# Sigmoid attention and a mixer MLP on one core: the third batch's cycles take the form of the later ones

## The chip, the core and the metric

The kernel runs on one core of a Trainium2 chip. The core has five engines that run side by side and meet at semaphores: TensorE (PE in the profile), which multiplies matrices and writes PSUM; VectorE (DVE) and ScalarE (ACT), which read PSUM and SBUF and compute element by element; GpSimd (POOL) and SyncE (SP), which here mostly start transfers. SBUF and PSUM have 128 partitions; PSUM holds eight banks of 512 f32 columns in each. The metric is the device time of one execution in microseconds (us); the median of several runs is given with its lowest and highest.

A matrix product here is written `matmul(out, lhsT, rhs)`: the weights `lhsT` are loaded into the array (at most 128 rows by 128 columns), then `rhs` streams through. Products of 64 rows by 64 columns occupy one quadrant of the array, and four of them in different quadrants run at once. The profile writes `64*64` or `128*128` for the two forms.

## The reference

Eight batches, twelve heads, 448 tokens, head size 64. Sigmoid attention, then one token-mixing and one channel-mixing MLP, each with a residual:

```python
scores = scale * np.matmul(q, k.transpose(0, 1, 3, 2)) - np.log(S)
attn = 1.0 / (1.0 + np.exp(-scores))
x = matmul(attn, v)                      # (8, 448, 768): heads side by side
h = np.maximum(x.transpose(0, 2, 1) @ w_tok1, 0.0) @ w_tok2   # over tokens, 256 wide
u = x + h.transpose(0, 2, 1)
out = u + np.maximum(u @ w_ch1, 0.0) @ w_ch2                  # over channels, 1536 wide
```

## The kernel before, in words

**Cycles.** The order of all instructions is written out by hand (a manual schedule); each engine executes its own instructions in that order. The unit of attention work is a *cycle* c = 3 b + u: batch b and one third u of its heads (four heads, in two groups g). There are 24 cycles, numbered from 0. A cycle holds seven score products `qk` (L179), each followed by a sigmoid on ACT (L191), and, one cycle later, the seven value products `av` (L201), whose result DVE casts into `xT` (L220) and SP transposes into `xn` by DMA (`xtrans_dma`, L235). Two cycles later the token MLP of that unit runs: `tok_tail` (L260) for the last 64 tokens, `tok1` (L278) for the other 384, a relu on ACT for each of its two halves (L303), and `ytrans` (L305), which multiplies by the second weight and adds x on DVE to give u, kept transposed in `uts`.

**Channel MLP.** Batch 0's first channel product (`ch1`) is spread over cycles 3 to 5. From batch 1 on it is `sevens` (L1049): seven products of sums and differences in place of eight plain ones, at the end of the third cycle of the next batch. It needs sums of the weight `c1` (`weight_sums`, L401: twelve DVE additions) and differences of u (`token_sums`, L422: four). Its seven products for three groups of outputs are named in `ORDER` (L1046); "2b" is the third step, and `banks` gives the banks for the single ones. The second channel product gives the output. Its 448 tokens are three blocks t of 128 and a last 64 (`ch2_last`, L722); each block has two halves of the 768 channels. A *group* is (t, half): twelve matmuls of 384 columns. For batch 0 the residual u is added on PE by three more matmuls with the identity (L552); for later batches u is transposed by DMA (`utrans`, L324) and added on DVE.

**Two forms of a cycle.** Cycles 6 to 8 (batch 2) are the loop at L1065. It puts batch 0's groups in whole-array form between the scores, a few matmuls at a time, from a list of pieces (`pending`) shared out by width (`work`, L1076). Cycles 9 to 23 are the loop at L1130. There a cycle's two groups, the two halves of one block of the batch two before, are a pair (`ch2_pair`, L582): eight of the twelve steps of both are done in quadrants (`quads`, L359), where the two row halves of the array work on different groups at a time and swap in the second turn, and the last four whole (`rest`, L602). So scores, pair, values and `tok_tail` are all 64x64 until the seventh score, and what follows (`tok1`, `rest`, `ytrans`, and in a batch's third cycle `ch2_last` and `sevens`) is 128x128.

**PSUM banks.** Scores and the larger products of `sevens` use two buffers of two banks each ("qk"). The other four banks, m0 to m3, are given out by `bank` (L85): in the opening by the string `OPENING_BANKS`, afterwards from `at_bank` upwards. The second loop gives the pair X = 2 and 3, and the values, then `tok_tail` and `tok1`, then `ytrans`, Y = 0 and 1; `ch2_last` takes Y + 1. In the first loop groups and `ch2_last` take 2 or 3. A tile that reuses a bank waits until its last reader is done.

**Queues.** `through_dma` (L144) prepares a batch's keys and queries: three DVE copies (`relayout`, L126) and one DMA transpose on SP for each. Such pieces wait in the list `copies`, and the loops take some of them off at set places (`some`, L1058; `within` and `behind` say how many). SP issues in order: transposes of x, keys, queries and u, and the stores of finished outputs (L577). POOL issues the loads. `gated_loads` (L969) lets POOL wait, by a copy that reads the transposed queries, before it loads keys, queries and values of later batches.

The opening, cycle 5 (L989) included, has its own loop; cycle 5 ends with two of batch 0's groups, (0, 0) and (1, 0), in whole-array form:

```python
for w, f in pieces_ch2(0, by_half[:2]):
    f()
    if copies:
        copies.pop(0)()
```

Of the kernel before, what the change touches and what calls it, by code (L numbers as in the profile page):

```python
# [10 lines left out]
FP32 = mybir.dt.float32  # L11
ADD = mybir.AluOpType.add
# [11 lines left out]
NU = 3  # L24
NS = 224
BY_GROUP = [0, 1, 6, 7, 2, 3, 8, 9, 4, 5, 10, 11]
OPENING_BANKS = "201301301301302130213021302130213130212130213021302021302"


@with_exitstack  # L30
def kernel(
# [53 lines left out]
    def bank(shape, dtype, name):  # L85

        if opening_banks:
            n = opening_banks.pop(0)
        else:
            n = at_bank[0]  # L90
            at_bank[0] = (n + 1) % 4
        return pp.tile(shape, dtype, tag=f"m{n}", bufs=1, name=name)
# [486 lines left out]
                in_=outs[b, t][64 * par : 64 * par + 64, :],  # L579
            )  # L580

    def ch2_pair(b, t):  # L582


        outs[b, t] = pa.tile([128, D], FP32, tag="outs", bufs=3, name=f"o_{b}_{t}")
        ps = [bank([128, 512], FP32, f"c2_{b}_{t}_{p}") for p in range(2)]
        n_quads = 8

        def step(turn, n):
            quads(  # L590
                ps,
                DH,
                turn,
                lambda p, part, m: h2[b][
                    part, BY_GROUP[n], 128 * t + m : 128 * t + m + 64
                ],
                lambda p, part: c2[part, BY_GROUP[n], DH * p : DH * p + DH],
                n == 0,
                False,
            )  # L600

        def rest():  # L602
            for p in range(2):
                for n in range(n_quads, NCB):
                    nc.tensor.matmul(  # L605
                        out=ps[p][:, 0:DH],
                        lhsT=h2[b][:, BY_GROUP[n], 128 * t : 128 * t + 128],
                        rhs=c2[:, BY_GROUP[n], DH * p : DH * p + DH],
                        start=False,
                        stop=(n == NCB - 1),  # L610
                    )
                ch2_out(b, t, p, ps[p])

        turns = [[lambda t=t, n=n: step(t, n) for n in range(n_quads)] for t in range(2)]
        return turns[0], turns[1], rest

    LOW, HIGH = slice(0, NCB // 2), slice(NCB // 2, NCB)
    D1, D2 = slice(0, DH), slice(DH, D)
# [234 lines left out]
    def pieces_ch2(b, groups):  # L853
        for t, half in groups:
            for n in range(0, NCB, 3):
                yield 3 * DH, lambda t=t, half=half, n=n: ch2(b, t, half, n, n + 3)

    def pieces_last(b):
        for n in range(0, NCB, 3):
            yield 3 * DH, lambda n=n: ch2_last(b, n, n + 3)  # L860
# [122 lines left out]

    ON_DMA = range(N_FIRST, N_CYCLES)

    ONE_RUN = 3 * NU

    by_half = sorted(((t, half) for t in range(3) for half in range(2)), key=lambda g: g[1])
    for c, cb in ((N_FIRST, 3), (N_FIRST + 1, 8)):  # L989
        b, u = divmod(c, NU)  # L990
        before = divmod(c - 1, NU)
        ahead = divmod(c + 1, NU)
        copies = []

# [24 lines left out]
        end()  # L1019
        qk(b, u, 6)  # L1020
        if u == 2:
            copies = by_unit(2, 1)
        whole(cb + 2)
        if c - 1 not in ON_DMA:
            xtrans(*before)
        for t in ("k", "q"):
            pe_transpose(ahead[0], t, ahead[1])
        whole(cb + 3)
        if c == N_FIRST:
            tok1(*before)  # L1030
            whole(cb + 4)
            nc.gpsimd.dma_start(out=w1[64:128, 3, :], in_=tok_rows[NJ - 1])
            ytrans(*before)
        else:
            for w, f in pieces_ch2(0, by_half[:2]):
                f()
                if copies:
                    copies.pop(0)()
            while copies:
                copies.pop(0)()  # L1040

            nc.gpsimd.tensor_copy(out=gate[:, :], in_=tr[2, "q"][:, 1, NJ - 1, 126:128])
            load(2, "v", v, 1, NU)
            gated_loads(b)
# [8 lines left out]
            if copies and at in (1, 3):  # L1053
                copies.pop(0)()

    pending, copies = [], []

    def some(n):  # L1058
        for f in copies[:n]:
            f()  # L1060
        del copies[:n]

    early = weight_sums()
    lane = [0]
    for c in range(2 * NU, ONE_RUN):  # L1065
        b, u = divmod(c, NU)
        before, ahead = divmod(c - 1, NU), divmod(c - 2, NU)


        if c == 2 * NU:  # L1070
            first = c
            pending, shares = [*pieces_ch2(0, by_half[2:]), *pieces_last(0)], [10, 10, 10]
            total = sum(w for w, f in pending)
            spent = 0

        def work(share):  # L1076
            goal = 3 * sum(shares[: c - first]) + share * shares[c - first]
            done = 0
            while pending and spent + done < total * goal / 90:
                w, f = pending.pop(0)  # L1080
                if len(pending) % 4 == 3:
                    lane[0] ^= 1
                at_bank[0] = 2 + lane[0]
                f()
                done += w
                if copies:
                    copies.pop(0)()
                elif early:
                    early.pop(0)()
            return done  # L1090

        some(len(copies))
        qk(b, u, 0)
        qk(b, u, 1)
        at_bank[0] = 0
        av(*before)
        xtrans_dma(*before)
        qk(b, u, 2)
        if c == 2 * NU + 2:
            copies += through_dma(3, 0)[NU + 1 :]  # L1100
        spent += work(1)
        qk(b, u, 3)
        qk(b, u, 4)
        if u < 2:
            at_bank[0] = 0
            tok_tail(*ahead)
            tok1(*ahead, with_scores=True)
        spent += work(2)
        if c == 2 * NU + 2:
            utrans(b - 1)  # L1110
            token_sums(b - 1)
        qk(b, u, 5)
        qk(b, u, 6)
        at_bank[0] = 0
        if u < 2:
            ytrans(*ahead)
        else:
            tok_tail(*ahead)
            tok1(*ahead, with_scores=True)
        if c == 2 * NU + 1:  # L1120
            copies += through_dma(3, 0)[: NU + 1]
        spent += work(3)
        if u == 2:
            sevens(b - 1)
            at_bank[0] = 0
            ytrans(*ahead)
            gated_loads(b)
    assert not copies and not pending and not early

    for c in range(ONE_RUN, N_CYCLES):  # L1130
        b, u = divmod(c, NU)
        before, ahead = divmod(c - 1, NU), divmod(c - 2, NU)
        if b == NU:
            within, behind = ((0, 0), (4, 2), (2, 0))[u]
        else:
            within, behind = ((0, 2), (2, 4), (0, 0))[u] if b < B - 1 else (2, 2)
        if u == 0:
            assert not copies
            copies += through_dma(b + 1, 0) if b + 1 < B else output_sums()

        X, Y = 2, 0
        at_bank[0] = X
        turn0, turn1, rest = ch2_pair(b - 2, u)
        part = len(turn1) * 2 // 3
        qk(b, u, 0)
        qk(b, u, 1)
        for f in turn0:
            f()  # L1150
        qk(b, u, 2)
        some(within)
        if c == ONE_RUN + 2:
            gated_loads(b)
        if u == 2:
            utrans(b - 1)
        at_bank[0] = Y
        av(*before, 0, 4)
        qk(b, u, 3)
        av(*before, 4, NJ)  # L1160
        xtrans_dma(*before)
        if u == 2:
            token_sums(b - 1)
        qk(b, u, 4)
        for f in turn1[:part]:
            f()
        qk(b, u, 5)
        for f in turn1[part:]:
            f()
        at_bank[0] = Y  # L1170
        tok_tail(*ahead)
        qk(b, u, 6)
        tok1(*ahead, with_scores=True)
        rest()
        if u == 2:
            at_bank[0] = Y + 1
            for w, f in pieces_last(b - 2):
                f()
            sevens(b - 1)
# [98 lines left out]
```

## Time and profile before

| What | Value |
|---|---|
| Median of 3 runs | 347.22 us (346.83 to 348.2) |
| The profiled execution | 347.06 us, span 345.3 us, granted TensorE clock 0.998 |
| PE busy | 337.6 us, 98% of the span |
| DVE busy, ACT busy | 213.3 us (62%), 210.5 us (61%) |
| POOL busy | 56.8 us (16%) |
| Cycle 5, from its first score matmul to that of cycle 6 | 50.95 to 64.03 us |
| Cycle 6 | 64.03 to 72.47 us |
| Cycle 7 | 72.47 to 81.08 us |
| Cycle 8, to the first of the seven products | 81.08 to 89.25 us |
| Seven products and `ytrans`, to cycle 9 | 89.25 to 102.18 us |
| Cycle 9 | 102.18 to 110.48 us |

The span goes from the first to the last instruction; the device time is a little longer. In the rows of the timeline the first number is the start, the second the length of the merged group, then engine, line, operation, what is written from what, the array form for matmuls, the shape, and the number of instructions; a bracket gives the idle time before and what ended it. Matmuls are pipelined and their ends are modelled, so a group's length runs into the next one: times between starts are the better measure. A line can be that of a helper.

### The profile page before, as it was taken

What the parts mean: (1) busy time and instruction counts of PE and PEld (TensorE: products, weight loads), DVE (VectorE), ACT (ScalarE), POOL (GpSimd) and SP (SyncE); (2) the same over time, 40 slices, a digit from 0 to 9 for tenths busy, and PEclk for the clock granted to TensorE, in tenths of its full rate; (3) what the DMA queues carried; (4) which work ended last, traced back from release to release, by engine and by line L of the source; (5) the groups of instructions that cost most, each with busy time, mean ns of one, the idle gap of its engine ahead of it and who ended that gap; (6) DMA issues with size and microseconds to landing.
All of it is one profiled execution on the core that took longest, in us unless ns stands there. A gap on an engine that the chain in (4) does not pass through costs nothing.

```text
span 345.3 us, 10253 instructions
## 1 busy us (share of the span) xinstructions
PE 337.6 (98%) x4465; PEld 238.5 (69%) x4465; DVE 213.3 (62%) x427; ACT 210.5 (61%) x271; POOL 56.8 (16%) x98
## 2 busy tenths in 40 slices
PE   7999999999999999999999999999999999999994
PEld 4555556555886669766896669766896669767962
DVE  2376466578574664657574664666665675976662
ACT  3996847488648865788448865688448875111400
POOL 8982440130040003000400004000100000000000
PEclk9999999999999999999999999999999999999999
DMA  8999999999999999969999999958992592035406
GB/s 127 158 170 194 209 203 203 173 185 233 199 180 194 189 172 206 164 104 168 182 155 175 161 163 209 184 104 159 178 146 34 78 173 66 1 78 129 78 2 159
DMA packets 104380, 52.17 MB, mean 151 GB/s; under 512 B 76432, under 2 KB 101264, under 8 KB 104336
## 3 DMA queue, kind: packets, MB, share of 16 engines
q1 hardware_dynamic: 78944, 29.70, 47.4%
q0 software_dynamic: 25168, 21.50, 42.1%
q8 instruction: 35, 0.57, 0.6%
q10 hardware_dynamic: 224, 0.33, 0.3%
q14 instruction: 9, 0.07, 0.1%
HBM read 43.45 MB, written 11.01 MB: 158 GB/s over the span
## 4 chain that ended last, share of the span: by engine, by line
PE 86%; DMA 5%; POOL 4%; ACT 2%; issue 1%; DVE 0%; ACTq 0%; POOLq 0%
PE c_ab L491 14%; PE c L367 12%; PE qk L184 8%; PE c_c L491 8%; PE xa L211 7%; PE c L541 6%; PE c L605 6%; PE yt L312 5%; PE tk L289 5%; PE c L734 5%; PE c L695 4%; DMA c<-in_moe_w_ch_dram 3%; PE c L344 3%; ACT att L191 2%; DMA w2s<-in_moe_w_tok_dram 2%
## 5 line engine op out<-in xcount | busy, mean ns | idle before, releaser
L191 ACT ACTIVATE att<-qk,att_bias 128x896 f16<-128x896 f32 x168 | 154.9, 1016 | 34.0 <-PE qk L184 33.6
L184 PE MATMUL qk<-tr_q,tr_k 64*64 64x448 f16 x672 | 58.1, 359 | 0.9 <-ACT att L191 0.6
L491 PEld LDWEIGHTS <-c 128*128 128x128 f16 x504 | 47.8, 98 | 1.9 <-issue 1.8
L220 DVE CAST xT<-xa 128x448 f16<-128x448 f32 x48 | 27.8, 620 | 32.5 <-PE xa L211 32.5
L367 PE MATMUL c<-c,h 64*64 64x384 f16 x960 | 46.6, 322 | 0.0
L211 PE MATMUL xa<-att,raw_v 64*64 64x448 f16 x672 | 39.5, 349 | 0.0
L512 ACT ACTIVATE pt_ab<-c_ab 128x896 f32<-128x896 f32 x21 | 19.3, 917 | 31.4 <-PE c_ab L491 30.2
L367 PEld LDWEIGHTS <-h 64*64 64x64 f16 x960 | 28.1, 107 | 11.9
L491 PEld LDWEIGHTS <-sum 128*128 128x128 f16 x378 | 36.3, 98 | 0.0
L184 PEld LDWEIGHTS <-tr_k 64*64 64x64 f16 x672 | 20.5, 105 | 20.7 <-issue 13.0
L564 DVE TENSOR_TENSOR o<-un,c 128x384 f32<-128x384 f16 x34 | 18.8, 554 | 23.8 <-PE c L605 20.4
L319 DVE TENSOR_TENSOR ut<-xT,yt 128x448 f16<-128x448 f16 x48 | 27.5, 615 | 3.0 <-PE yt L312 3.0
L211 PEld LDWEIGHTS <-raw_v 64*64 64x64 f16 x672 | 20.2, 107 | 10.9 <-issue 0.3
L971 POOL COPY gate<-tr_q 128x2 f16<-128x2 f16 x6 | 1.1, 190 | 153.5 <-DMA tr_q<-rel_q 153.5
L303 ACT ACTIVATE h<-tk 128x256 f16<-128x256 f32 x42 | 14.4, 415 | 14.8 <-PE tk L289 14.8
L541 PE MATMUL c<-c,h 128*128 128x384 f16 x120 | 22.3, 326 | 0.0
L312 PE MATMUL yt<-w,h 128*128 128x448 f16 x96 | 22.1, 353 | 0.0
L605 PE MATMUL c<-c,h 128*128 128x384 f16 x120 | 22.0, 326 | 0.0
L514 ACT ACTIVATE h<-c_ab 128x896 f16<-128x896 f32 x7 | 6.4, 917 | 24.4 <-PE c_ab L491 24.4
L289 PE MATMUL tk<-xn,w 128*128 128x256 f16 x156 | 21.2, 274 | 0.1
L521 DVE TENSOR_TENSOR h<-pt_ab,c_ab 128x896 f16<-128x896 f32 x14 | 15.2, 1084 | 9.6 <-PE c_ab L491 9.6
L521 DVE TENSOR_TENSOR h<-pt_c,c_c 128x448 f16<-128x448 f32 x21 | 13.0, 617 | 12.4 <-PE c_c L491 12.4
(100 smaller groups left out, 458.7 us busy)
## 6 DMA issues: line engine op xcount, KB each, us to landing
out_dram<-o SPq DMA_DIRECT2D x48, 192.0 KB, 2.8
c<-in_moe_w_ch_dram POOLq DMA_DIRECT2D x4, 1152.0 KB, 15.8
raw_k<-in_k_dram POOLq DMA_DIRECT2D x10, 336.0 KB, 8.7
raw_q<-in_q_dram POOLq DMA_DIRECT2D x10, 336.0 KB, 13.0
raw_v<-in_v_dram POOLq DMA_DIRECT2D x10, 336.0 KB, 11.0
out_dram<-o SPq DMA_DIRECT2D x15, 96.0 KB, 7.2
raw_q<-in_q_dram POOLq DMA_DIRECT2D x12, 112.0 KB, 5.3
raw_k<-in_k_dram POOLq DMA_DIRECT2D x12, 112.0 KB, 5.1
```

What stands on the lines that cost most here:

```text
L184: nc.tensor.matmul(out=ps[64 * g : 64 * g + 64, hi, 0:S], lhsT=tr[b, "k"][64 * hi : 64 * hi + 64, u, j, 64 * g : 64 * g + 64], rhs=tr[b, " ...
L191: nc.scalar.activation(out=att[b, u, j][:, :, :], in_=ps[:, :, 0:S], func=SIGMOID, bias=bias_t[:, :], scale=att_scale,)
L211: nc.tensor.matmul(out=ps[g][64 * hi : 64 * hi + 64, 0:S], lhsT=raw[b, "v"][64 * g : 64 * g + 64, u, hi, j, :], rhs=att[b, u, j][64 * g : ...
L220: nc.vector.tensor_copy(out=xTs[b % 2][:, u, g, 0:S], in_=ps[g][:, 0:S])
L289: nc.tensor.matmul(out=ps[tcb], lhsT=w1[rows, t, cols], rhs=xn[b, u][rows, :, t, :], start=(t == 0 and not with_scores), stop=(t == (2 if ...
L312: nc.tensor.matmul(out=ps[:, 0:S], lhsT=h1[b, u][:, tcb, g, :], rhs=w2[:, tcb, :, :], start=(tcb == 0), stop=(tcb == 1),)
L319: nc.vector.tensor_tensor(out=uts[b % 2][:, db, 0:S], in0=xTs[b % 2][:, u, g, 0:S], in1=ps[:, 0:S], op=ADD)
L367: nc.tensor.matmul(out=ps[p][m : m + 64, 0:n], lhsT=lhsT(p, part, m), rhs=rhs(p, part), start=(first and turn == 0), stop=(last and turn = ...
L491: nc.tensor.matmul(out=ps[:, g, p, :], lhsT=weights[n][:, d, 128 * cb : 128 * cb + 128], rhs=moving[n][:, d, :], start=(n in (1, 5, 2) and ...
L521: nc.vector.tensor_tensor(out=shaped(dst), in0=shaped(parts[gs, which]), in1=ps, op=ADD)
L541: nc.tensor.matmul(out=ps[:, 0:DH], lhsT=h2[b][:, BY_GROUP[cb], 128 * t : 128 * t + 128], rhs=c2[:, BY_GROUP[cb], cols], start=(cb == 0), ...
L605: nc.tensor.matmul(out=ps[p][:, 0:DH], lhsT=h2[b][:, BY_GROUP[n], 128 * t : 128 * t + 128], rhs=c2[:, BY_GROUP[n], DH * p : DH * p + DH], ...
```

## The change

Cycles 6 to 8 move into the second loop (`ONE_RUN` is now 2 * NU); the first loop, with `pending` and `work`, goes. Cycle 5 does group (0, 0) alone. Cycle 6 has the pair of groups (1, 0) and (2, 0), cycle 7 the pair (0, 1) and (1, 1), and `ch2_pair` now takes a list of groups. Cycle 8 has one group left, (2, 1): the new `ch2_split` does all its twelve steps in quadrants, the two row halves into a bank each, and DVE copies one and adds the other. The residual of batch 0 is added on PE as before (`u_on_pe`). The weight sums are taken from `copies`, three at a time, in cycles 6 and 7; the keys' relayout and transpose for batch 3 come in cycle 8 after the third score, the queries' after the group's output, followed by `utrans` and `gated_loads`. `ch2_last` of batch 0 takes bank Y + 1.

```diff
-OPENING_BANKS = "201301301301302130213021302130213130212130213021302021302"
+OPENING_BANKS = "20130130130130213021302130213021313021213021302130202130"
...
+    def u_on_pe(b, t, half, ps):
+        for n in range(0 if b in un else NU):
+            nc.tensor.matmul(
+                out=ps[:, 128 * n : 128 * n + 128],
+                lhsT=uts[b % 2][:, NU * half + n, 128 * t : 128 * t + 128],
+                rhs=ident[:, :],
+                start=False,
+                stop=(n == NU - 1),
+            )
+
+    def ch2_pair(b, groups):
+
+        for t, half in groups:
+            opened(b, t)
+        ps = [bank([128, 512], FP32, f"c2_{b}_{t}_{half}") for t, half in groups]
         n_quads = 8
...
-                        stop=(n == NCB - 1),
+                        stop=(n == NCB - 1 and b in un),
                     )
-                ch2_out(b, t, p, ps[p])
+                u_on_pe(b, *groups[p], ps[p])
+                ch2_out(b, *groups[p], ps[p])
...
+    def ch2_split(b, t, half):
+
+        opened(b, t)
+        ps = [bank([128, 512], FP32, f"c2_{b}_{t}_{half}_{r}") for r in range(2)]
+        cols = slice(DH * half, DH * half + DH)
+
+        def step(n):
+            for r in range(2):
+                part = slice(64 * r, 64 * r + 64)
+                for m in (0, 64):
+                    nc.tensor.matmul(
+                        out=ps[r][m : m + 64, 0:DH],
+                        lhsT=h2[b][part, BY_GROUP[n], 128 * t + m : 128 * t + m + 64],
+                        rhs=c2[part, BY_GROUP[n], cols],
+                        start=(n == 0),
+                        stop=(n == NCB - 1 and (r == 1 or b in un)),
+                    )
+
+        def rest():
+            u_on_pe(b, t, half, ps[0])
+            o = outs[b, t][:, cols]
+            nc.vector.tensor_copy(out=o, in_=ps[0][:, 0:DH])
+            nc.vector.tensor_tensor(out=o, in0=o, in1=ps[1][:, 0:DH], op=ADD)
+            store(b, t)
+
+        steps = [lambda n=n: step(n) for n in range(NCB)]
+        return steps[: NCB // 2], steps[NCB // 2 :], rest
...
-    ONE_RUN = 3 * NU
+    ONE_RUN = 2 * NU
...
-            for w, f in pieces_ch2(0, by_half[:2]):
+            for w, f in pieces_ch2(0, [(0, 0)]):
...
-    early = weight_sums()
-    lane = [0]
-    for c in range(2 * NU, ONE_RUN):
...
     for c in range(ONE_RUN, N_CYCLES):
         b, u = divmod(c, NU)
         before, ahead = divmod(c - 1, NU), divmod(c - 2, NU)
-        if b == NU:
+        if b == 2:
+            within, behind = ((3, 3), (3, 3), (4, 0))[u]
+        elif b == 3:
             within, behind = ((0, 0), (4, 2), (2, 0))[u]
         else:
             within, behind = ((0, 2), (2, 4), (0, 0))[u] if b < B - 1 else (2, 2)
         if u == 0:
             assert not copies
+            if b == 2:
+                copies += weight_sums()
             copies += through_dma(b + 1, 0) if b + 1 < B else output_sums()
...
-        turn0, turn1, rest = ch2_pair(b - 2, u)
+        if b > 2:
+            turn0, turn1, rest = ch2_pair(b - 2, [(u, 0), (u, 1)])
+        elif u < 2:
+            turn0, turn1, rest = ch2_pair(0, ([(1, 0), (2, 0)], [(0, 1), (1, 1)])[u])
+        else:
+            turn0, turn1, rest = ch2_split(0, 2, 1)
...
-        if c == ONE_RUN + 2:
+        if c == 3 * NU + 2:
             gated_loads(b)
-        if u == 2:
+        if u == 2 and b > 2:
             utrans(b - 1)
...
         rest()
+        if u == 2 and b == 2:
+            some(4)
+            utrans(b - 1)
+            gated_loads(b)
         if u == 2:
             at_bank[0] = Y + 1
             for w, f in pieces_last(b - 2):
```

More of the change, by code (lines that the diff above doesn't have):

```diff
@@ L580, in store, with opened, tokens, cols @@
             )
-    def ch2_pair(b, t):
-        outs[b, t] = pa.tile([128, D], FP32, tag="outs", bufs=3, name=f"o_{b}_{t}")
-        ps = [bank([128, 512], FP32, f"c2_{b}_{t}_{p}") for p in range(2)]
-        n_quads = 8
+    def opened(b, t):
+        if (b, t) not in outs:
+            outs[b, t] = pa.tile([128, D], FP32, tag="outs", bufs=3, name=f"o_{b}_{t}")
+    def u_on_pe(b, t, half, ps):
[11 more added lines that the diff above has]
+        ps = [bank([128, 512], FP32, f"c2_{b}_{t}_{half}") for t, half in groups]
+        n_quads = 8
+        def tokens(p, m=0, n=128):
+            at = 128 * groups[p][0] + m
+            return slice(at, at + n)
+        def cols(p):
+            return slice(DH * groups[p][1], DH * groups[p][1] + DH)
         def step(turn, n):
@@ L593, in step @@
                 turn,
[L594 to L597, printed above, removed]
+                lambda p, part, m: h2[b][part, BY_GROUP[n], tokens(p, m, 64)],
+                lambda p, part: c2[part, BY_GROUP[n], cols(p)],
                 n == 0,
@@ L606, in rest @@
                         out=ps[p][:, 0:DH],
-                        lhsT=h2[b][:, BY_GROUP[n], 128 * t : 128 * t + 128],
-                        rhs=c2[:, BY_GROUP[n], DH * p : DH * p + DH],
+                        lhsT=h2[b][:, BY_GROUP[n], tokens(p)],
+                        rhs=c2[:, BY_GROUP[n], cols(p)],
                         start=False,
-                        stop=(n == NCB - 1),
+                        stop=(n == NCB - 1 and b in un),
                     )
-                ch2_out(b, t, p, ps[p])
+                u_on_pe(b, *groups[p], ps[p])
+                ch2_out(b, *groups[p], ps[p])
         turns = [[lambda t=t, n=n: step(t, n) for n in range(n_quads)] for t in range(2)]
         return turns[0], turns[1], rest
+    def ch2_split(b, t, half):
[21 more added lines that the diff above has]
+        return steps[: NCB // 2], steps[NCB // 2 :], rest
     LOW, HIGH = slice(0, NCB // 2), slice(NCB // 2, NCB)
@@ L1054, in sevens @@
                 copies.pop(0)()
-    pending, copies = [], []
+    copies = []
     def some(n):
@@ L1061, in some @@
         del copies[:n]
-    early = weight_sums()
-    lane = [0]
-    for c in range(2 * NU, ONE_RUN):
[L1066 to L1122, printed above, removed]
-        if u == 2:
[L1124 to L1128, printed above, removed]
     for c in range(ONE_RUN, N_CYCLES):
```

1 line of the change is left out of this document (removed).

## The prediction

> **What bounds the kernel now.** I read the page first: its table of engines and its chain of waits. TensorE (PE) is busy for 98% of the span and carries 86% of the chain, so a change counts only if it alters what PE executes or makes PE wait.
>
> ```profile
> PE 86%; DMA 5%; POOL 4%; ACT 2%; issue 1%; DVE 0%; ACTq 0%; POOLq 0%
> ```
>
> Then the busy times by stretch, cut at the first score matmul of cycles 5, 6, 7, 8, at the first matmul of the seven products, and at cycles 9, 10, 11. After the times the columns are length, then busy time and instruction count of PE, weight loads, DVE, ACT and POOL, then the granted clock (1.00 throughout).
>
> ```profile
> 50.95:64.03 13.08, 12.99 (x175) 8.03 (x175) 8.44 (x16) 6.40 (x7) 0.54 (x1) 1.00 1.29 194
> 64.03:72.47 8.44, 8.44 (x96) 4.45 (x94) 6.03 (x13) 7.10 (x9) 3.00 (x7) 1.00 1.24 168
> 72.47:81.08 8.61, 8.61 (x98) 4.83 (x98) 6.77 (x15) 7.17 (x10) 1.31 (x2) 1.00 1.29 199
> 81.08:89.25 8.17, 7.70 (x107) 4.38 (x106) 6.81 (x14) 7.12 (x10) 0.00 (x0) 1.00 1.14 246
> ...
> 102.18:110.48 8.30, 8.30 (x143) 5.28 (x142) 3.76 (x9) 6.95 (x9) 0.00 (x0) 1.00 1.26 209
> 110.48:118.80 8.32, 8.32 (x143) 5.20 (x143) 5.11 (x11) 6.95 (x9) 0.00 (x0) 1.00 1.17 191
> ```
>
> PE has no gap in cycles 6 and 7 and idles 0.47 us in cycle 8; ACT needs about 7 us per cycle whatever PE does. Next, PE in order of time: in cycle 6 (the old form), in cycle 9 (the form that cycles 6 to 8 get) and at the end of cycle 11.
>
> ```profile
> 65.76 0.36 PE L184 MATMUL qk<-tr_q,tr_k 64*64 64x448 f16 x4
> 66.05 1.64 PE L541 MATMUL c<-c,h 128*128 128x384 f16 x9
> 67.61 0.57 PE L184 MATMUL qk<-tr_q,tr_k 64*64 64x448 f16 x8
> ...
> 102.58 1.47 PE L367 MATMUL c<-c,h 64*64 64x384 f16 x32
> 103.89 0.36 PE L184 MATMUL qk<-tr_q,tr_k 64*64 64x448 f16 x4
> ...
> 108.33 1.46 PE L605 MATMUL c<-c,h 128*128 128x384 f16 x8
> 109.63 0.92 PE L312 MATMUL yt<-w,h 128*128 128x448 f16 x4
> ...
> 124.95 1.46 PE L605 MATMUL c<-c,h 128*128 128x384 f16 x8
> 126.34 2.14 PE L734 MATMUL c<-c,h 128*64 128x384 f16 x24
> ```
>
> Then ACT in cycle 11, which starts at 118.80:
>
> ```profile
> 119.30 6.40 ACT L191 ACTIVATE att<-qk,att_bias 128x896 f16<-128x896 f32 x7 [1.43 <-PE qk L184]
> 125.54 0.70 ACT L303 ACTIVATE h<-tk 128x256 f16<-128x256 f32 x2
> ```
>
> And two kinds of DVE work that the change moves or that stand in its way, in cycle 8 and after it:
>
> ```profile
> 80.90 1.66 DVE L126 COPY rel_k<-raw_k 128x896 f16<-128x896 f16 x3
> ...
> 89.36 1.14 DVE L757 COPY o<-c 64x384 f32<-64x384 f32 x2 [0.92 <-PE c L745]
> ```
>
> What to see, by starts (pipelined ends overlap): 32 quadrant matmuls of 384 columns take 1.31 us (102.58 to 103.89) and eight whole ones 1.30 (108.33 to 109.63). They do the same arithmetic, so splitting into quadrants costs nothing in itself. Going from 64x64 to 128x128 costs 0.10 (65.76 to 66.05 is 0.29, four score matmuls take 0.19), and so does going back (nine matmuls from 66.05 end at 67.51, the next starts at 67.61). Cycle 6 goes over and back three times, cycle 9 once.
>
> **The change part by part.** Tn is the start of cycle n.
>
> *Cycle 5, one group less.* In PE's order of time the first group's last matmuls start at 61.65 and the next group starts at 61.82; the second group's start at 63.77 and cycle 6 at 64.03. Without the second group cycle 6 starts at 61.82 + 0.09 = 61.91: minus 2.12.
>
> *Cycles 6 and 7.* They get the form of cycles 9 and 10 (8.30, 8.32), plus the residual on PE: three 128-column matmuls per group, 0.17 by starts (61.65 to 61.82), so 0.33. That gives 8.63 and 8.65, against 8.44 and 8.61 with 21 group matmuls each. T7 = 70.54, T8 = 79.19. Of the 0.4 a cycle that the two saved switches bring, none is visible in these lengths, because each now carries 24 group matmuls (three more, 0.49).
>
> *Cycle 8.* Only half a pair is left: 48 quadrant matmuls, 1.95 us of work where cycle 11 has 3.90. So ACT becomes the limit. Its nine operations run back to back in cycle 11 from +0.50 to +7.44, and none of them leaves. PE reaches the end of the token matmuls at +6.15 (124.95 less 118.80), adds 0.17 of residual, and then wants bank 1 for the last 64 tokens (at_bank = Y + 1). The token result of the second half lies in that bank until ACT's second relu: +7.44. In cycle 11 eight whole matmuls (1.30) cover this time almost exactly, the next group starting 0.10 after the relu; here the cover is 0.17. In the kernel before, the last group took bank 2 or 3 and had no such wait. So it starts at +7.54, as in cycle 11, takes 2.08 (126.34 to 128.42) and 0.27 of residual, and the seven products start at +9.89 instead of 8.17.
>
> *Sum.* Before: 13.08 + 8.44 + 8.61 + 8.17 = 38.30. After: 10.96 + 8.63 + 8.65 + 9.89 = 38.13. From the seven products on, the order is the same and PE has no gap up to 141.35, so the shift passes to the end: minus 0.17.
>
> *DVE, with weight sums and relayouts moved.* Cycle 6: three sums before the casts of av's result fit while av still runs. Cycle 7: two residual additions of cycle 6 until +0.8, six weight sums at 0.505 (two from 70.22 to 71.23) until +3.83 where av's last matmuls end near +3.4; the casts (1.19 for two) end at +5.0, and the next user of their banks comes at +5.09. Cost: nothing, or up to 0.2. Cycle 8: additions until +0.8, three sums until +2.3, three k relayouts (1.66) until +3.9, casts and tail until +5.24, four differences (2.01, from 86.43 to 88.44) until +7.25, the split group's copy 0.47 and addition (0.55 by the row of f32 plus PSUM) until +8.2, three q relayouts until +9.84. The seventh score needs the casts done by +5.3 to stay ahead of ACT (its turn is at +5.84). The two copies of the last group, 1.14, start when PE is done, near +10.05, and end at +11.1. The product 2b, which takes bank 1 back, starts 1.73 after the first product (89.25 to 90.98): +11.62. Margin 0.5, cost nothing; if DVE ran x later, x less 0.5. It has no idle time in these ten microseconds.
>
> *SP and POOL* (landing times from the list of transfers). The k transposes of batch 3 go at T8 + 3.9 = 83.1 (before 82.63). Behind them wait the transposes of x (needed in cycle 9) and two stores, then the q transposes at about 89.4 (before 89.11), then u's. The q transposes took 6.2 to land, so 95.6, with cycle 9 at 102.0; u's took 8.1, so 102, used by the first output near 109. POOL's gate waits for q as before (95.45), and its loads are some 0.2 later: values land by 105, needed near 112. Nothing on the path.
>
> *Early need.* Cycle 6 asks for the tokens of cycle 4 and the last weight rows at 61.91 + 5.09 = 67.0, a microsecond earlier than before (68.02). Both landed at 66.1 (55.91 + 10.2 and 53.19 + 12.9). Margin 0.9.
>
> The profiled execution took 347.06, with 345.3 of span; the median is 347.22, 0.16 higher. So 346.89 on its own scale, 347.05 on the median's; I say 347.0.
>
> **The rivals.**
>
> *PE ends cycle 8 (faster).* If the relu did not hold bank 1, PE would start the last group at +6.32 instead of +7.54: 1.22 less, 345.8. For it: six round trips of 0.2 are really removed, and the 0.47 gap with them. Against: the bank numbers in the code and ACT's unbroken 6.94 us.
>
> *DVE ends cycle 8 (slower).* The q relayouts stand ahead of the copies that free bank 1. It decides from 0.5 us of DVE lateness; to be slower than before takes 0.7. Bounds: nothing by the durations above; if all three relayouts came after the copies' due time, 1.66 less 0.5 = 1.16, so 348.2. Against: DVE is free at +9.84, PE needs it at +10.05. The Trainium skill, TensorEngine Tiling (Array Packing), Performance Considerations, says that tiling speeds up TensorE and not the emptying of PSUM, which can become the bottleneck; by it this rival would win, while in cycles 9 and 10, fully tiled, DVE is busy for 3.76 and 5.11 of 8.3 us, which does not bear it out there.
>
> *A transfer ends last (slower).* Tokens or weight rows later than 67.0 hold cycle 6 one for one. Landings of such transposes spread from 3.1 to 10.2 us, so up to 2 us late is thinkable: 348 to 349. Against: they start before anything differs.
>
> **How the numbers follow.** Forecast 0.72 (own range 346.4 to 347.6: the 0.2s above to either side and the spread of the runs); PE-ended 0.12; DVE-ended 0.11; transfer 0.05. Half a per cent is 1.7 us, about what a measurement of this kernel tells from no change. The forecast lies inside it; the faster rival reaches 1.4, so 0.06 beyond; the slower ones pass it in 0.08. Range 345.8 to 348.0: it leaves out half of the faster rival and most of the transfer.
>
> **What would show it.** Cycle 6 starting near 61.9; cycles 6 and 7 near 8.6; in cycle 8 a PE gap of about a microsecond ahead of the last 64 tokens, released by the relu; the seven products near 89.1; cycle 9 near 102.0. Wrong if that gap is missing (faster), or if PE waits for DVE inside the products or at the token matmuls, or for DMA in cycle 6 (slower).

## The result

The changed kernel is slower in the first comparison: median 349.37 us (346.5 to 352.22, 21 runs) against 347.22 (345.41 to 349.43, 21 runs), ratio 1.0048, 95% interval 1.0025 to 1.0071. A later comparison on another occasion gave 348.43 (345.47 to 352.25, 12 runs) against 347.18, ratio 0.9993 (0.9957 to 1.0029). The ratios in this document leave out runs more than 1.5% above the fastest of their kernel: in the second comparison these are the changed kernel's three longest, which its median counts, so that 0.9993 understates the loss. Neither number says much without the runs themselves, which fall apart into two kinds:

```
changed, 21 runs:  346.5 346.6 346.9 346.9 | 348.4 348.4 348.5 348.7 348.8 348.9
                   349.4 349.5 349.7 349.8 350.1 350.2 350.2 350.5 350.7 350.7 352.2
changed, 12 runs:  345.5 346.5 346.6 346.7 346.8 347.7 | 349.2 349.3 350.0 350.7 351.2 352.3
before, 21 runs:   17 between 345.4 and 347.8; 348.0 348.2 348.9 349.4 (rounded)
```

Ten of the changed kernel's 33 runs lie between 345.5 and 347.7, around the forecast of 347.0; the other 23 lie 1.4 to 5.3 us above it. The kernel before has long runs too, but fewer: over all comparisons of this document 11 of its 102 runs are above 349, up to 352.53, against 17 of these 33. The half clock that is shown below is not in all of the long runs: in six of the 23, among them 350.06 and 350.22, the granted clock is 0.999 or 1.000. The profiled execution of the changed kernel took 352.22, the longest of the first 21, with a span of 350.5. A second trace of the same kernel, from a run of 346.49 with a span of 344.7, is set beside it; together they show the two kinds. "x of cycle n" below is the tile that SP sends to be transposed in cycle n and that the token product of cycle n + 1 reads; the prediction's "tokens of cycle 4" are the x of cycle 5.

### The profile after

The chain of waits on the page, first of the long run, then of the short one (one fence for each). Before it was PE 86%, DMA 5%.

```profile
PE 80%; DMA 12%; POOL 4%; ACT 2%; issue 1%; DVE 0%; ACTq 0%; POOLq 0%
```

```profile
PE 89%; ACT 6%; issue 2%; DMA 1%; DVE 1%; ACTq 0%; DVEq 0%
```

Busy times by stretch, cut as in the prediction at the starts of cycles 5, 6, 7, 8 and at the first of the seven products: the long run, then the short run, which goes on to cycle 9.

```profile
50.75:61.72 10.97, 10.88 (x161) 6.69 (x161) 7.89 (x15) 6.40 (x7) 0.54 (x1) 1.00 1.29 201
61.72:70.64 8.92, 8.82 (x150) 5.50 (x148) 4.51 (x10) 7.02 (x9) 0.49 (x2) 1.00 1.27 152
70.64:79.28 8.64, 8.64 (x150) 5.67 (x149) 6.26 (x14) 6.95 (x9) 4.08 (x7) 1.00 1.10 165
79.28:94.50 15.22, 10.88 (x149) 7.14 (x148) 9.84 (x20) 7.17 (x9) 0.00 (x0) 0.78 1.21 199
```

```profile
50.72:61.68 10.96, 10.87 (x160) 6.69 (x159) 7.88 (x15) 6.39 (x7) 0.53 (x1) 1.00 1.29 202
61.68:70.32 8.64, 8.64 (x151) 5.66 (x149) 4.52 (x10) 6.94 (x9) 2.14 (x5) 1.00 1.20 176
70.32:78.96 8.64, 8.64 (x152) 5.67 (x151) 6.25 (x14) 6.94 (x9) 2.10 (x4) 1.00 1.19 185
78.96:88.68 9.72, 8.70 (x149) 6.23 (x148) 9.58 (x20) 6.94 (x9) 0.00 (x0) 1.00 1.10 219
88.68:101.61 12.93, 12.93 (x133) 12.38 (x130) 8.25 (x17) 5.82 (x8) 4.26 (x7) 1.00 0.99 174
```

In the short run the four lengths are 10.96, 8.64, 8.64 and 9.72, where the prediction has 10.96, 8.63, 8.65 and 9.89; cycle 9 starts 50.89 after cycle 5, before 51.23. In the long run cycle 8 takes 15.22, of which PE is busy for 10.88, and the clock column has 0.78 (1.00 is full speed). PE in order of time shows what lies in it, here the token product of cycle 8 (L270, L289), the residual (L588), the last 64 tokens (L782, L793) and the first of the seven products, in the long run and then in the short one:

```profile
83.72 0.52 PE L647 MATMUL c<-c,h 64*64 64x384 f16 x8
88.42 0.43 PE L270 MATMUL tk<-xn,w 64*64 64x256 f16 x4 [4.18 <-DMA xn<-xT]
88.63 0.59 PE L184 MATMUL qk<-tr_q,tr_k 64*64 64x448 f16 x4
89.15 1.46 PE L289 MATMUL tk<-xn,w 128*128 128x256 f16 x6
90.41 0.53 PE L588 MATMUL c<-ident,ut 128*128 128x128 f16 x3
91.09 3.31 PE L782 MATMUL c<-c,h 128*64 128x384 f16 x24 [0.15 <-ACT h L303]
94.21 0.36 PE L793 MATMUL c<-ident,ut 128*64 128x128 f16 x6
94.50 1.32 PE L491 MATMUL c_ab<-ut,c 128*128 128x224 f16 x12
```

```profile
83.71 0.61 PE L270 MATMUL tk<-xn,w 64*64 64x256 f16 x4
84.10 0.41 PE L184 MATMUL qk<-tr_q,tr_k 64*64 64x448 f16 x4
84.44 0.83 PE L289 MATMUL tk<-xn,w 128*128 128x256 f16 x6
85.11 0.33 PE L588 MATMUL c<-ident,ut 128*128 128x128 f16 x3
86.44 2.14 PE L782 MATMUL c<-c,h 128*64 128x384 f16 x24 [1.00 <-ACT h L303]
```

The long run waits 4.18 us for `xn`, the x of batch 2's first unit, which SP sent to be transposed in cycle 7: the x of cycle 7. And after the wait everything is slow: the 24 matmuls of the last 64 tokens take 3.12 by starts (91.09 to 94.21), in the short run 1.95 (86.44 to 88.39). The clock says why. The long run in stretches of 2 us, the clock after POOL's column; it falls while PE still waits (0.67 from 86 to 88, where PE has no work) and is full again from 94:

```profile
84.00:86.00 2.00, 0.24 (x8) 0.00 (x0) 1.97 (x6) 1.28 (x2) 0.00 (x0) 1.00 1.55 88
86.00:88.00 2.00, 0.00 (x0) 0.00 (x0) 1.68 (x4) 0.00 (x0) 0.00 (x0) 0.67 0.91 241
88.00:90.00 2.00, 1.58 (x13) 0.80 (x14) 0.00 (x0) 0.67 (x1) 0.00 (x0) 0.50 1.22 238
90.00:92.00 2.00, 1.85 (x12) 1.31 (x12) 0.99 (x2) 1.00 (x3) 0.00 (x0) 0.50 1.25 279
92.00:94.00 2.00, 2.00 (x18) 1.52 (x16) 1.70 (x4) 0.00 (x0) 0.00 (x0) 0.62 1.01 193
94.00:96.00 2.00, 2.00 (x28) 1.85 (x24) 1.11 (x2) 0.14 (x1) 0.00 (x0) 1.00 1.55 197
```

From the start of the token product to the seven products the long run needs 6.08 us with 0.15 of waiting for the relu (88.42 to 94.50), the short one 4.97 with 1.00 (83.71 to 88.68): 5.93 against 3.97, so the half clock costs 1.96. The sum for cycle 8 is then 9.72 + 4.39 (token product later) + 1.96 - 0.85 (less waiting for the relu) = 15.22. The other new wait is 0.28 in cycle 6 (8.92 against 8.64), at the same operation: its weight load waits 0.47 for the x of cycle 5, issued at 55.71 and landed 11.3 later.

When did this transfer land? The list of transfers gives the time from issue to landing. In the kernel before it was issued at 75.85, in the long run at 75.78:

```profile
xn<-xT SPq DMA_TRANSPOSE x1, 6.7
```

```profile
xn<-xT SPq DMA_TRANSPOSE x1, 12.6
```

So it landed near 82.5 and 88.4. The kernel before asks for it at 86.99, where its token product of cycle 8 stands, with 2.26 us of work behind it until the seven products:

```profile
86.99 0.30 PE L270 MATMUL tk<-xn,w 64*64 64x256 f16 x4
87.22 0.83 PE L289 MATMUL tk<-xn,w 128*128 128x256 f16 x6
87.98 1.17 PE L734 MATMUL c<-c,h 128*64 128x384 f16 x12
89.25 1.32 PE L491 MATMUL c_ab<-ut,c 128*128 128x224 f16 x12
```

The changed kernel asks at about 84. A second trace of the kernel before has 75.99 + 6.4 = 82.4, the short run of the changed kernel 75.46 + 7.2 = 82.7. What moves in that time can be counted from the trace's packets, by start, in KB per microsecond; "loads" are POOL's queue (values of batch 2, keys and queries of batch 3), "SP" are transposes and stores:

```
us            72  73  74  75  76  77  78  79  80  81  82  83  84  85  86  87
before loads 102  21 202 196 200 198 195 191 139   4   0   0   0   0   0   0
       SP     90 162   3   0   0   0   0   4  43 245 378 344 131 123 284 198
long   loads  10 144 179 158 176 165 172 187 163 102 132 123  20  32  22   7
       SP      4   0   0   0   0   0   0   2  24  30  36  52  18 104  82 361
short  loads 179 198 200 202 186 197 197 166  66   4   0   0   0   0   0   0
       SP      0   0   0   0   0   0   0  28 117 157 378 315 150 118 283 151
```

The transpose is issued near 75.8 in all three. Its packets hardly move while the loads run, and then slowly until these are through. Before and in the short run the loads are through by 81; in the long run they start 2 to 3 us later and trickle until 87, and x with them.

### The profile page after: what moved, and what is told of

The parts are those of the page before. It is cut to its first block, busy times and chain, and to the rows that moved or that the text cites. A ratio compares the mean times of both kernels' runs of the same rounds, so it can differ in the third digit from the quotient of the medians.

```text
span 350.5 us, 10516 instructions
## 1 busy us (share of the span) xinstructions
PE 337.8 (96%) x4597; PEld 241.5 (69%) x4597; DVE 213.9 (61%) x428; ACT 210.2 (60%) x271; POOL 57.2 (16%) x98
## 4 chain that ended last, share of the span: by engine, by line
PE 80%; DMA 12%; POOL 4%; ACT 2%; issue 1%; DVE 0%; ACTq 0%; POOLq 0%
PE c_ab L491 14%; PE c L367 12%; PE c_c L491 8%; PE qk L184 7%; DMA xn<-xT 7%; PE xa L211 6%; PE c L624 6%; PE c L782 5%; PE tk L289 5%; PE yt L312 5%; PE c L743 4%; DMA c<-in_moe_w_ch_dram 3%; PE c L541 2%; PE c L344 2%; ACT att L191 2%; DMA w<-in_moe_w_tok_dram 2%
## 5 line engine op out<-in xcount | busy, mean ns | idle before, releaser
L367 PE MATMUL c<-c,h 64*64 64x384 f16 x1088 | 52.9, 322 | 0.0
L367 PEld LDWEIGHTS <-h 64*64 64x64 f16 x1088 | 31.8, 107 | 13.5
L184 PEld LDWEIGHTS <-tr_k 64*64 64x64 f16 x672 | 21.6, 105 | 19.6 <-issue 11.6
L624 PE MATMUL c<-c,h 128*128 128x384 f16 x136 | 25.2, 326 | 0.0
L289 PE MATMUL tk<-xn,w 128*128 128x256 f16 x156 | 21.8, 279 | 0.1
L521 DVE TENSOR_TENSOR h<-pt_c,c_c 128x448 f16<-128x448 f32 x21 | 12.9, 616 | 12.6 <-PE c_c L491 12.6
L289 PEld LDWEIGHTS <-w 128*128 128x128 f16 x156 | 13.9, 99 | 7.4 <-issue 5.3
```

What stands on the lines that cost most here:

```text
L184: nc.tensor.matmul(out=ps[64 * g : 64 * g + 64, hi, 0:S], lhsT=tr[b, "k"][64 * hi : 64 * hi + 64, u, j, 64 * g : 64 * g + 64], rhs=tr[b, " ...
L289: nc.tensor.matmul(out=ps[tcb], lhsT=w1[rows, t, cols], rhs=xn[b, u][rows, :, t, :], start=(t == 0 and not with_scores), stop=(t == (2 if ...
L367: nc.tensor.matmul(out=ps[p][m : m + 64, 0:n], lhsT=lhsT(p, part, m), rhs=rhs(p, part), start=(first and turn == 0), stop=(last and turn = ...
L521: nc.vector.tensor_tensor(out=shaped(dst), in0=shaped(parts[gs, which]), in1=ps, op=ADD)
L624: nc.tensor.matmul(out=ps[p][:, 0:DH], lhsT=h2[b][:, BY_GROUP[n], tokens(p)], rhs=c2[:, BY_GROUP[n], cols(p)], start=False, stop=(n == NCB ...
```

## The experiments

Theory A: PE comes to the token product of cycle 8 earlier than before, x lands when the loads let it, and a wait there costs twice, once itself and once through the clock. Theory B: a bank or an engine (the relu wait, DVE's queue) costs the time.

### The changed kernel again

No edit.

> The changed kernel once more, nothing edited. Theory A (PE waits in cycle 8 for the transposed x of batch 2's first unit, which lands late behind the loads of batch 3's keys and queries): times between 346.5 (landed in time) and 351, and in the trace a gap ahead of the token product of cycle 8, ended by that transfer. Theory B (the bank held by the relu, or DVE's queue, costs the time): about 349 in every run with no gap of more than 1.3 us at the token product.

Measured: the twelve runs above. Its trace is the short run: no gap at the token product, and 1.00 us of waiting for the relu. The relu wait is there in a run of 346.49, so it is not what makes the kernel slower: B falls for that part.

### Without the loads that stand in the way

```diff
+        if b == 1:
+            for t in ("k", "q"):
+                raw[3, t] = raw[2, t]
-        if b + 2 < B:
+        elif b + 2 < B:
             load(b + 2, "k", k, 0, NU)
...
-        if b + 2 < B:
+        if b != 1 and b + 2 < B:
             load(b + 2, "q", q, 0, NU)
```

> Leaves out the loads of batch 3's keys and queries (batch 2's are used again, so batch 3's output is another); everything else of the changed kernel stays. Theory A: the transposed x of cycle 7 lands in some 4 us instead of 12.6, no gap at the token product of cycle 8, 346.5 to 347.0, the 1.2 us wait for the relu ahead of the last 64 tokens remains. Theory B: no better than the changed kernel, 349.

Measured: 346.71 (345.68 to 348.11, 12 runs), ratio 0.9977 (0.9951 to 1.0003). The same transpose, issued at 75.70, by the list of transfers:

```profile
xn<-xT SPq DMA_TRANSPOSE x1, 3.0
```

3.0 us instead of 6.4 to 12.6 in the traces with the loads, and no wait in cycle 8. Here the loads that are left are through at 75.6, before the transpose is issued, and its first packet moves at 76.87, 1.2 us after its issue; with the loads the first one moves at 79.3 to 79.8. What remains at the token product is 0.65 in cycle 7, for the x of cycle 6. The loads are what the transpose waits for.

### x transposed on PE

```diff
+        if before != (2, 0):
-        xtrans_dma(*before)
+            xtrans_dma(*before)
...
         ytrans(*ahead)
+        if before == (2, 0):
+            at_bank[0] = X
+            xtrans(*before)
```

> The x of batch 2's first unit is transposed on PE at the end of cycle 7 (eight matmuls, 0.5 us by starts) and copied by DVE (0.69) instead of by DMA; the loads stay as they are. Theory A: no gap at the token product of cycle 8; 346.7 plus 0.5 for the transposes, 347.0 to 347.5. Theory B: 349.5.

Measured: 347.14 (346.52 to 347.6, 12 runs), ratio 0.9981 (0.9953 to 1.0009). The waits of PE in its trace (total, times, longest):

```profile
PE heat L920 <- DVE att_bias L839: 1.1, 1, 1.1
PE c L782 <- ACT h L303: 1.0, 1, 1.0
PE tp_q L167 <- DVE raw_q L933: 0.8, 1, 0.8
PE c L647 <- DVE xn L250: 0.6, 1, 0.6
PE qk L184 <- ACT att L191: 0.2, 1, 0.2
```

The loads are as they were, only the transfer is not needed, and not one of twelve runs goes above 347.6, where the changed kernel, timed on the same occasion, ranges up to 352. This shows that what the changed kernel loses in cycle 8, it loses to this one transfer. It doesn't show that every long run waits there: this kernel also comes to cycle 10 later, its token product there standing at 115.82, in the short run at 115.11. The price: 0.54 on PE and 0.6 in the next cycle, whose pair wants bank 2 back from DVE.

### The token product later

Here `late` is true in cycle 8.

```diff
-        tok_tail(*ahead)
+        if not late:
+            tok_tail(*ahead)
         qk(b, u, 6)
-        tok1(*ahead, with_scores=True)
+        if not late:
+            tok1(*ahead, with_scores=True)
         rest()
-        if u == 2 and b == 2:
-            some(4)
-            utrans(b - 1)
-            gated_loads(b)
...
             for w, f in pieces_last(b - 2):
                 f()
+            if late:
+                some(4)
+                utrans(b - 1)
+                gated_loads(b)
+                at_bank[0] = X
+                tok_tail(*ahead)
+                tok1(*ahead, with_scores=True)
             sevens(b - 1)
```

> In cycle 8 the token product is moved behind the last 64 tokens, just ahead of the seven products, into banks 2 and 3; so x is asked for 3 us later and the last 64 tokens no longer wait for the relu. Theory A with the relu wait as predicted: the gap goes or shrinks below 1.5 us in most runs and the relu's 1.2 us goes too: 345.7 to 346.5 where x has landed. If only the transfer mattered and the relu wait cost nothing: 346.7. Theory B with DVE as the cause: no change, 349.

Measured: 348.85 (345.95 to 351.14, 12 runs), ratio 1.0034 (0.9998 to 1.0069). A miss in the time, though both waits of cycle 8 are gone from its trace: x, issued at 74.58, took 9.3 and landed at 83.9, and the token product stands at 86.05. The stretch from cycle 6 to cycle 9 is 39.36 (60.81 to 100.17), in the short run 39.93 (61.68 to 101.61). The time went two cycles on:

```profile
113.07 0.66 PE L367 MATMUL c<-c,h 64*64 64x384 f16 x12
116.25 0.30 PE L270 MATMUL tk<-xn,w 64*64 64x256 f16 x4 [2.53 <-DMA xn<-xT]
116.39 0.36 PE L184 MATMUL qk<-tr_q,tr_k 64*64 64x448 f16 x4
116.68 0.86 PE L289 MATMUL tk<-xn,w 128*128 128x256 f16 x6
117.34 2.76 PE L624 MATMUL c<-c,h 128*128 128x384 f16 x8
```

Cycle 10 waits 2.53 us for the x of cycle 9, and then eight matmuls that take 1.30 elsewhere take 2.55 by starts (117.34 to 119.89). The same transfer, two cycles on: 11.0 us from issue to landing here, 8.3 before.

### Useless work ahead of the wait

```diff
+        if c == 2 * NU + 2:
+            pad = bank([128, 512], FP32, "pad")
+            for n in range(9):
+                nc.tensor.matmul(
+                    out=pad[:, :], lhsT=ident[:, :], rhs=c1[:, 0, 0:512], start=True, stop=True
+                )
+            at_bank[0] = Y
         tok_tail(*ahead)
```

> The changed kernel with nine useless whole-array matmuls of 512 columns (1.92 us, and about 0.2 for the change of form) ahead of the token product of cycle 8; results as before. Theory A (PE comes early to a transfer that it then waits for, and a long wait halves the clock afterwards): the runs that reached 346.5 rise to 347.5 to 348.5, part of the added work lying where PE waited for the relu; those that waited stay or fall, so the median is no higher than the changed kernel's 348.4 to 349.4, and the runs lie closer together. Theory B (PE, DVE or ACT bound throughout): the changed kernel's median plus 1 to 2, about 350.5.

Measured: 348.72 (348.0 to 349.34, 12 runs), ratio 1.0039 (1.0014 to 1.0064). 2 us of work added, and the median lies between the changed kernel's two medians, 348.43 and 349.37, of other occasions; the slowest run is 2.9 us faster than the slowest without the padding, 352.25, and the shortest rises from 345.47 to 348.0. In its trace x landed 11.3 after its issue at 75.87, so as late as 87.2, and PE waits 0.85 for it instead of some 3; the last 64 tokens take 2.24 (89.43 to 91.67) as with a full clock.

```profile
84.26 2.12 PE L1164 MATMUL pad<-c,ident 128*128 128x512 f16 x9
87.22 0.30 PE L270 MATMUL tk<-xn,w 64*64 64x256 f16 x4 [0.85 <-DMA xn<-xT]
88.31 0.33 PE L588 MATMUL c<-ident,ut 128*128 128x128 f16 x3
89.43 2.14 PE L782 MATMUL c<-c,h 128*64 128x384 f16 x24 [0.79 <-ACT h L303]
91.67 1.32 PE L491 MATMUL c_ab<-ut,c 128*128 128x224 f16 x12
```

### The kernel before with less work

Nine of twelve matmuls of group (1, 0) are left out in cycle 5.

```diff
...
-                start=(cb == 0),
+                start=(cb == (9 if (b, t, half) == (0, 1, 0) else 0)),
...
-            for n in range(0, NCB, 3):
+            for n in range(9 if (b, t, half) == (0, 1, 0) else 0, NCB, 3):
```

> The kernel before with nine of the twelve matmuls of group (1, 0) left out in cycle 5 (so that part of batch 0's output is another): 1.46 us less on PE, transfers as they were. Theory A with its second half (the transposed x of cycle 9 lands just when cycle 10 asks for it, so time saved ahead of cycle 10 is given back there): 346.8 to 348, with a PE wait of about 1.5 us for that transfer in cycle 10 or some in cycle 8, and more spread than before. If PE alone bounds this stretch: 345.7.

Measured: 346.72 (344.98 to 352.49, 12 runs), ratio 0.9979 (0.9948 to 1.0009). 1.46 us less on PE lower the median by 0.26, and the runs spread over 7.5 us. The trace happens to be the shortest run, 344.98, and has no such wait, so the expected wait in cycle 10 is not shown here. The best run is 0.8 below the best of its comparison, the longest as long as any; where the long ones waited is not known.

### The queries behind x

```diff
-        if b + 2 < B:
+        if b > 2 and b + 2 < B:
             load(b + 2, "q", q, 0, NU)
+
+    def load_q_behind_x(b, x):
+        nc.gpsimd.tensor_copy(out=gate[:, :], in_=xn[x][:, 1, 3, 126:128])
+        load(b, "q", q, 0, NU)
...
         xtrans_dma(*before)
+        if before == (2, 0):
+            load_q_behind_x(3, before)
+        if before == (2, 2):
+            load_q_behind_x(4, before)
```

> The changed kernel with the loads of the queries of batches 3 and 4 held back until the transposed x of cycle 7 and of cycle 9 has landed; the same bytes, another order. Theory A: both transposes land some 3 us earlier, no wait for them in cycles 8 and 10, 346.3 to 346.9 with little spread. If other transfers delay them as much: no change, 348.4 to 349.4.

> The same with the token product of cycle 8 behind the last 64 tokens as well, which took away the relu wait (cycle 9 came 1.4 us earlier). Theory A: 345.2 to 345.8. If the time saved is given back at another transfer: 346.5 or more, with a PE wait that names it.

Measured: 354.68 (351.39 to 356.17, 6 runs), ratio 1.0181 (1.0131 to 1.023), and 353.41 (352.79 to 355.11, 6 runs), ratio 1.0162 (1.0122 to 1.0201). Clear misses: neither expectation came. Values and keys alone kept the transpose waiting until 81.8 (76.31 + 5.5), and only then did the queries start. The waits of DVE name the new one:

```profile
DVE rel_q L126 <- DMA raw_q<-in_q_dram: 7.1, 2, 5.3
```

The relayout of the queries waits for its load, 1.85 in cycle 8 and 5.3 in cycle 11, and the casts queued behind it hold PE. Holding transfers back in a stretch that is short of transfer time moves the wait and adds to it.

### A second trace of the kernel before

No edit, one run: 347.58.

> The kernel before, nothing edited, for a second trace of it. Theory A: x of cycle 7, issued near 76, lands between 82 and 88 as in the other traces, and the token product of cycle 8 asks for it near 87, so that PE waits for it for less than 1.5 us or not at all.

The transpose landed at 82.4 and the token product of cycle 8 stands at 87.12 without a wait, as expected. In cycle 10, though, PE waits for the x of cycle 9, issued at 107.38 and landed 8.7 later:

```profile
116.10 0.30 PE L270 MATMUL tk<-xn,w 64*64 64x256 f16 x4 [0.23 <-DMA xn<-xT]
```

So the kernel before has no margin at all at that place in this run, and whatever is saved ahead of it can be lost there, as the run with the later token product showed.

### Both together

`pe_one_late` has x of cycle 7 transposed on PE, ahead of `ytrans`, and the token product of cycle 8 behind the last 64 tokens (the two edits above); `pe_two_late` transposes the x of cycle 9 on PE too.

> The changed kernel with the x of cycle 7 transposed on PE (ahead of the addition's product, in bank 2, 0.5 us) and the token product of cycle 8 behind the last 64 tokens (1.2 us less). Theory A: no wait in cycle 8; the 1.2 us come up against the x of cycle 9 in cycle 10, as in the run with the token product moved alone: 346 in some runs, 347.5 to 349 in others. If only cycle 8's transfer matters: 345.8 to 346.3 in nearly all.

> The same with the x of cycle 9 transposed on PE too, so that neither cycle 8 nor cycle 10 waits for a DMA transpose. Theory A: 346.0 to 346.6 with little spread, 0.2 to 0.3% below the kernel before. If the stretch is bound by transfers as a whole, another wait takes their place (keys or queries of batch 4, or x of cycle 10) and it stays near 347.

Measured: 346.19 (344.96 to 347.43, 12 runs), ratio 0.9963 (0.9938 to 0.9988), and 346.68 (345.87 to 347.8, 12 runs), ratio 0.9972 (0.9949 to 0.9995). The first is faster than the kernel before by 0.4% (0.1 to 0.6), its slowest run is below every long run of the changed kernel, and it does not fall apart into two kinds. Against x on PE alone (347.14, on another occasion) the later token product brings 0.95, about what the wait for the relu took. Its trace is of a run of 346.98, above its median, with 0.36 of waiting for x in cycle 6. The second's median is 0.49 higher, about the price of one more transpose on PE (0.54). It lies above the 346.0 to 346.6 that were expected, and the split of the first into 346 and 347.5 to 349 did not come.

## Why the prediction was wrong

**What held.** The sum of PE's work. Cycle 5 lost 2.1 us (10.96), cycles 6 and 7 take 8.64 (8.63 and 8.65 forecast), the quadrants cost nothing in themselves, and in the short run the last 64 tokens wait for the relu exactly where it was said: the wait ends at +7.48 from cycle 8's start (+7.54 forecast), 1.00 us (1.2 forecast). DVE's walk through cycle 8 came out within 0.25: the query relayouts run from +8.13 to +9.8, the copies of the last group from +9.82, and the product 2b does not wait. So DVE does not end cycle 8 in that trace, and PE does not end it either. The Trainium skill, TensorEngine Tiling (Array Packing), section PSUM Bottleneck, names the emptying of PSUM as what may become the bottleneck when the array is tiled; it did not here. Up to cycle 9 the short run gains 0.34 (50.89 for 51.23), where 0.17 was forecast. The runs of 346.5 to 346.9, four of the first 21, are the forecast.

**What failed.** The step *Early need*. It looked for transfers that PE now asks for earlier, and named one, in cycle 6, with a margin of 0.9. The same question was never put for cycles 7 and 8, though the trace of the kernel before had all the numbers: PE asks for x at about T8 + 5, that is 84, where the kernel before asks at 86.99, and the transpose was issued at 75.85 and landed 6.7 later, 82.5. The margin went from 4.5 to 1.6 us, and in cycle 10 there was next to none from the start (0.23 of waiting in the second trace of before). The step *SP and POOL* then listed what comes behind the key transposes and ended with "Nothing on the path": x of cycle 7 was not in the list because its issue did not move. It did not have to move; its reader did.

Even 1.6 us would have been enough by one profile. What was missing is that a landing is not a property of the transfer. With the loads in the way it came at 82.4 to 88.4 in the traces of the two kernels, some 0.6 to 1.4 us after the end of the loads, and the prediction took the one trace's value as fixed. Its rival of a late transfer, at 0.05 and placed in cycle 6, had the mechanism ("hold cycle 6 one for one") and was argued away with "they start before anything differs", which is true and no help: the changed kernel's margin is what differs. In cycle 6 itself it came true in the long run, at 0.28 us: the x of cycle 5 landed at 67.0, where the prediction has 66.1.

**What the wait costs.** The prediction priced a late transfer one for one. The trace has 4.18 us of waiting followed by 1.96 of matmuls at half the clock. The place of the wait costs as well. Without waits the changed kernel needs 3.97 us from the token product to the seven products, the kernel before 2.26, since it does more of the other work ahead of the token product. So, as an estimate from these rows, with a landing at 88.4 the kernel before would wait 1.4 and start the seven products near 90.7, the changed one at full clock near 92.4; the trace has 94.50. That is how a run can be slower than before rather than equal, and 1.7 of the 3.8 us do not need the half clock. The six long runs at full clock fit this, but none of them has a trace.

**What stays open.** Why the loads are through by 81 in one run and by 87 in the next. They start when POOL's gate sees the transposed queries of cycle 7, at 67.64 before and 70.10 in the long run (67.66 in the short run); what held these queries up was not tested. Nor is it known in how many of the long runs the wait was in cycle 8 and in how many in cycle 10.

## What to carry to other kernels

When a change makes the bounding engine arrive earlier anywhere, list every transfer that it reads from there on, with its landing and the margin before and after, and not only the transfers that the change moves. Count also the work that stands behind each such wait: it is what a late landing holds back. A landing time from one profile is one draw: look at what else the DMA engines carry at that time, and take the end of that traffic, and a microsecond or so more (0.6 to 1.4 here), as its bound. Runs that fall apart into two groups point to a wait that is sometimes there; removing the dependence (here a transpose on PE for one tile, 0.5 us) can be worth more than the work that it costs.

## What the runs showed of the hardware

- A DMA transpose from SP's queue hardly moves while POOL's queue has large loads: nothing from its issue at 75.8 until after 79, where without the loads its first packet moves 1.2 us after the issue; then some 30 to 50 KB per us beside the loads, and 245 once they are done (the kernel before at 81, stores included); 3.0 us in all without two of the loads, 12.6 at worst with them. The Trainium skill, DMA: Bandwidth & Descriptors, section Queues, rings and completion order, says that each engine takes turns between its queues packet by packet; the packets here agree with that only in the mixed stretch, not before 79.
- A wait of PE of 2.53 us (cycle 10 of the run with the later token product) was followed by half the clock, after PE had started again at 116.25: the clock was 1.00 from 112 to 116, 0.83 from 116 to 118, 0.50 from 118 to 120 and 0.81 from 120 to 122. The Trainium skill, TensorE: Matmul & The Clock Gate, section HAM oscillation, gives idle gaps above about 3.4 us as the danger; here a shorter one did it. After the wait of 4.18 in the long run it was otherwise: there the clock fell within the wait. A wait of 0.85 (the run with useless work) left it at 1.00.

```profile
114.00:116.00 2.00, 0.00 (x0) 0.00 (x0) 0.73 (x3) 0.41 (x1) 0.00 (x0) 1.00 1.03 229
118.00:120.00 2.00, 2.00 (x8) 0.99 (x7) 0.55 (x1) 0.41 (x2) 0.00 (x0) 0.50 1.73 195
```

- Two microseconds of useless matmuls in front of a wait left the median where it was, took 2.9 us off the slowest run (352.25 to 349.34) and added 2.5 to the shortest (345.47 to 348.0).
